# Late loads in fewer, larger pieces without ties, and a new order of work planned with later transpose landings

## The chip, the cores and the metric

The kernel runs on one core of a Trainium2 chip. A core has a matrix engine (TensorE, PE in the profile), a vector engine (VectorE, DVE), an activation engine (ScalarE, ACT), a general engine (GpSimd, POOL) and a queue engine (SyncE, SP) that issues transfers; 16 DMA engines carry them. The metric is the device time of one execution in microseconds (us); smaller is better.

## The reference

One transformer block on a sequence of S = 2048 rows of D = 448 values, in bf16. Six vectors come out of the condition `c`; they shift, scale and gate a memory attention and a gated feed-forward network (FFN). Cut to what matters:

```python
mod = (silu(c) @ w_mod).reshape(1, 6, 1, 448)            # sa, ca, ga, sb, cb, gb
h = layernorm(x) * (1 + ca) + sa
# attention: 16 heads of 28, the sequence in N = 4 segments of L = 512
for s in range(4):
    p = softmax(qs @ ks.T * scale + causal_mask)
    a_dot = p @ vs
    a_mem = (phi(qs) @ M) / (phi(qs) @ z + 1e-6)         # phi(t) = t + 1 if t > 0 else exp(t)
    o = g * a_mem + (1 - g) * a_dot                      # g = sigmoid(beta) of the head
    M = M + phi(ks).T @ vs;  z = z + sum(phi(ks))
x = x + ga * (o @ wo)
h = layernorm(x) * (1 + cb) + sb
x = x + gb * ((sigmoid(h @ w_gate) * (h @ w_up)) @ w_down)   # F = 1792
```

## The kernel before

**Staging.** Everything stays on the core. Rows of x are kept as 16 tiles of 128 rows; four tiles make one segment. Activations that feed a matmul are turned so that the feature lies on the partitions: `hT` holds a segment of the normed input, `qT` and `kT` the projections, `fT` the gated FFN values. A segment passes through `ln1` (layer norm and turning), `proj` (q, k, v), `attention` (logits L962, exponential L976 and L982, causal mask L989 and L992, PV L1017, then `unit`'s vector work), `memory` (phi of k, its transpose L917, the update of M by L925), `wo_ln2` (output projection L1084, second layer norm) and `ffn` (gate and up L1106, tanh L1111, product L1113, down L1125, residual L1132, store L1134).

**Turning.** Segments 1 and 2 of the first layer norm (and segment 0) are turned on TensorE (`turned`). Segment 3 and every second layer norm are turned by DMA transposes on SP (`transposed`, L766), and then two DMA copies, `below` (L783) and `above` (L786), bring the second half-layout of `hT`. `memory` turns phi(k) by a DMA transpose on SP (L917) for segments 0 to 2.

**The order of work is planned.** The kernel first builds a graph of nodes (`add`), one for each group of instructions, with an engine or several possible ones, a duration in ns, its dependencies, and the ring slots it takes and frees. `Graph.run` then walks through time and gives every engine its instructions in a fixed order: of the nodes that are ready, the one with the greatest rank (longest planned path to the end) plus a priority from the table `PRM` goes first. `COST` weighs the durations when a node may go to one of several engines, and `STAY` is a bonus for matmuls of the same kind as the last. On the chip each engine runs its list in that order, and waits where an input is not there yet. What the planner believes only shapes the order; no instruction waits for a planned time.

**The planner's belief about transfers.** A node with `move` bytes extends a modelled queue per issuing engine (`moved`, 215 bytes per ns alone, 111 shared); its result counts as landed when that queue is through, plus `LAND` (800 ns), plus the node's own `lag`. `ready_at` can hold a load of over 100 KB back while the modelled queue is more than `BACKLOG` ahead; at 1e9 it never does. Where the plan leaves TensorE idle, `fillers` adds matmuls that compute nothing needed (L1149), one for each 215 ns of a gap beyond `SLACK`.

**Loads.** The first group (x of segments 0 and 1, w_mod's first two blocks, wq, wk, wv) is issued in a fixed order at the start. The "late" loads follow, all on SP: x of segments 2 and 3, wo, beta, the other four blocks of w_mod, gate and up weights, down weights. They are cut into pieces of mostly 196 to 229 KB. From the 13th load on (`UNTIED`), a load is tied to the third load before it (`DEPTH`): the instruction on SP waits until that one has landed. `ld()` hands out the priorities of the late loads.

```python
        tie = loads[-DEPTH] if len(loads) >= UNTIED else None
        n = add(eng, 450 if size < 200000 else 640, fn, [*deps, tie], prio=prio, use=use, take=take, move=size, lag=lag)
        n.tie = tie
```

**Other names.** `ot` is the ring in which a finished tile of 128 rows waits for its store. w_mod's later blocks are loaded into the `fT` ring's space, blocks 3 and 4 first in it, then 2, then 5; block 2 gives ga, which scales wo (L679, then L757), block 5 gives gb, which scales w_down.

Of the kernel before, what the change touches and what calls it, by code (L numbers as in the profile page):

```python
# [7 lines left out]
BF16 = mybir.dt.bfloat16  # L8
# [5 lines left out]
P = 128  # L14
# [5 lines left out]
BACKLOG = 1e9  # L20
SLACK = 250
# [4 lines left out]
    "ld": (771, 403768, 348483, 259726, 535371, -278835, -292028, 445172, 1332362, 303233, 1310460, 45242, 288244,  # L26
        -128559, 1040237, 258096, -9990, 569649, 1024340, 391761, 273500, 593899, 795982, -203552, 820620, 593017,
        1120207, 330985, 1113461, 774493, -671071, -90668, 539398, 799422, -93184, 23288, -674131, 254991),
    "ws": (-14005, -102989, -62310, -137580, -381981, -699688, -219766, -155414, -94849, -10346, -123259, -3702,
        29063, -36253, -322382, -40930, -239067, -199319),  # L30
    "pj": (-280142, -704069, -638572, -518614, -637310, -994157, -542144, -688882, -109480, 161573, -1121205, 12951,
        -402680, -604681, -789625, -528195, 72916, -492335, 12521, -313241, -475423, 372917, -235992, -493897, 610722,
        658204, 321509, 693085, -400674, -1003709, -194017, 106939, 222219, -486884, 47564, 827879, -632040, 544043,
        -11321, -249733, 478544, -452337, -133586, 492909, 126034),
    "ev": (1516111, 1582287, 1138122, 640813, 1428776, 707733, 1221781, 1425071, 1717384, 1397734, 1614980, 1052150,
        1134267, 1025622, 1180727, 2207166, 1378057, 854006, 1335199, 930050, 1372900, -496693, -46859, 1361141,
        -498332, -673866, 39791, -625676, -211702, -535966, 79681, 418783, -341986, -1205310, -1102479, -1758438,
        -859392, -1109485, -955341, -758887, -1106561, -1044137, -935118, -1085307, -583137, -511278, -1028157,
        -1225711),
    "ln1": (1014613, 259455, 311242, 526284, -532656, 377084, 521927, 458915, 248468, 240899, 80767, 190939, 322045,  # L40
        922394, -153714, 373880, 672893, 684073, 1312461, 646485, 525704, 132711, 142935, 229741, -119849, -25882,
        -1076, 59463, 99488, 4145, 203011, -9620, 36748, -275452, -42630, -532745, 127715, 337951, 124107, 234908,
        173169, 1026151, 293341, -767251, 146664, 291291, -294982, -141991, -214427, -355224, -804385, -231165,
        265245, -289951, 78489, -14810, -607527, 273452, 95473, -109467, -145027, 816731, 184508, -257527, 422111),
    "lg": (3531987, 2928887, 3302070, 2312646, 1981257, 2222351, 1556422, 2079865, 2540545, 1674238, 496386, 1265056,
        644299, 1008454, 803464, 213638, 548428, 1112707, 740179, 279054, 724651, 615799, 812429, 1475696, 1307754,
        581830, 466619, 1033964, 1156072, 857527, 674454, 450311, 546011, 1045955, 595283, 1128384, 850233, 464085,
        496739, 861364),
    "ex": (1660442, 1247168, 1466499, 1378343, 1124806, 556127, 1086877, 940357, 360731, 688715, 2399920, 1680821,
        1560577, 1033906, 1812669, 1303255, 2255484, 2297242, 1801796, 344197, -105916, 575997, 217295, 364760,  # L50
        -144111, 34843, 947142, -243088, -712255, 146737, 1249995, 1295152, 802692, 1243758, 2446324, 1105808,
        1108368, 816977, 1361359, 686920),
    "mask": (2833694, 2172153, 1484862, 2558992, 2745471, 1943529, 1669348, 1566800, 2360084, 2108728, 1848729,
        1771049, 1289664, 2173349, 1689570, 1032184, 372083, 533670, 1070582, 530111, 517237, 567036, 334578, 644150,
        1017921, 1097020, 1263687, 1004873, 761044, 578011, 988940, 1329620, 772189, 530798, 366834, 656439, 773092,
        -452969, 460512, 344381, -382752, 248779, 43481, 1005712, 1163774, 187316, 918710, 863964, -364060, -57999,
        225822, 119677, 455905, 353891, 573582, -336115, 142521, 6226, 871244, 334930, 617018, 447958, 306715,
        823560),
    "pv": (1510960, 2254349, 2150147, 892491, -81679, 241060, 567421, 807042, 479666, 494468, -63278, -109593,
        -365197, -45904, -144814, -682418),  # L60
    "t": (2245238, 2091550, 1479107, 2357610, 2278955, 1940928, 1941447, 2463059, 2054908, 1760115, 1657910, 1666629,
        1715318, 2114714, 1290324, 1855182, 714137, 1869659, 2188586, 1895895, 277605, 932172, 144282, 369456, 432516,
        370017, 275497, -66930, 79936, -66111, 155980, 490864, 995475, 377538, -769977, -593018, 161869, -266693,
        -79670, 112558, 887899, -388864, -721366, -451132, 403656, 179168, 5328, 541028, 1289320, 876258, 1495114,
        1300857, 1661961, 359418, 1176846, 1749849, 530354, 579482, 1179131, 667989, 1127818, 1398569, 890064, 868091,
        1217557, 751753, 1166194, 723957, 1026257, 725394, 1350910, 1100815, 783159, 905073, 764601, 1017372, -918149,
        -347294, -688818, 277986, -73264, -342300, -1164722, -373929, -494748, -249055, -693970, -808798, -932705,
        -1317168, -144432, -1300560, -467191, -376473, -198986, -768635, -951192, -1164539, -833366, -860480, -847331,
        -1205016, -1112039, -972589),
    "mem": (75524, -45857, 9188, 551184, 145444, 51132, 382367, -354439, -82631, 339528, -85643, -352126, -37850,  # L70
        79814, -226912, -49579, 34854, -204535, 646779, -2750, 26526, -54116, 149438, -67183, -123127, -205995,
        551520, -232370, 21817, -17851, 23659, 117299, -297990, -59887, -870756, -180055, 24537, 125755, -319961,
        -313276, 43719, -4031, -195138, 24147, -179664, 373048, 200012, -375, 313049, 240205, -216959, 38022, 78802,
        107419, 111432, 455670, -378853, 59098, 139550, -259246, 424659, -747222, 670979, -62528, 15753, -81855,
        -113175, 2765, -557394, -377468, 395418, 196975, -443658, 319806, -286386, -254599, 284180, 432906, 363582,
        742822, -378872, -14501, 367698, 73066),
    "wo": (1928953, 1133983, 1813540, 2305809, 864403, 1645199, 1747926, 1593145, 691139, 732374, 496645, -54449,
        -926050, 953596, 300390, -140998),
    "ln2": (1235442, 1377352, 1905298, 772371, 1302459, 1454679, 1592833, 713116, 1440875, 1339697, 1170368, 1293312,
        1828436, 1147645, 1699501, 1313252, 1150856, 1235422, 878015, 2046656, 2294705, 2027521, 2032455, 1793018,  # L80
        1744547, 1152936, 853562, 625765, 1526373, 647445, 916507, 962776, 889384, 1328237, 1212566, 918603, 665248,
        648263, 1674146, 408683, 1295773, 1318265, 1064317, 1357524, 885031, 702760, 1493860, 1125808, 819020,
        1311131, 956359, 526544, -1247537, -1766227, -1030854, -1340553, -1669186, -1740353, -1452415, -1159770,
        -847930, -933910, -1364788, -1142350, -1477850, -806597, -1686672, -1416655, -1223326, -1150467, -1728888,
        -1160041, -1823461, -1614144, -1601250, -1685498, -2399938, -1489365, 1616614, 1988001, 2192457, 1853517,
        2476805, 2921069, 1730775, 2573100, 2277872, 2889185, 2711768, 2000762, 2913408, 2496652, 2218550, 2856210,
        2811230, 3473453, 2544526, 2779098, 2604614, 2132813, 2981200, 2286328, 3348949, 2656893),
    "gu": (2673986, 2907356, 2967087, 2529995, 3263422, 2686764, 2603478, 2577456, 1978393, 2148466, 1618981, 1176658,
        2204195, 3478258, 1852084, -121925, 261498, 636554, 209114, 416027, 31833, 498183, 874090, 115018, 221051,
        681715, 442901, 777503, 745824, 803670, -198195, -7556, 1161045, 117077, 681087, 874132, 152642, 541639,  # L90
# [22 lines left out]
        -396451, -551498, -486620, -45176, -808892, -509914, -384534, -367362, -583030, -515930),  # L113
}
STAY = 69838
COST = {"ACT": 0.956, "DVE": 0.949, "POOL": 0.819}


class Slot:
# [225 lines left out]
def kernel(  # L345
# [362 lines left out]
    def ld():  # L708
        return pr("ld", 0)
# [473 lines left out]
```

## Time and profile before

| | us |
|---|---|
| median of 3 runs | 262.75 (261.62 to 262.83) |
| the profiled execution | 261.97 |
| its span, first to last instruction | 260.3 |
| TensorE's mean granted clock | 0.985 |

Busy time of the engines by line, as the profile's groups give it (one row for all shapes of a line's operation):

| line, engine, what | count | busy us | mean ns |
|---|---|---|---|
| L1106 PE gate and up | 784 | 92.3 | 377 |
| L1125 PE down | 224 | 46.3 | 353 |
| L881 PE q and k | 224 | 28.8 | 386 |
| L1149 PE fillers | 14 | 3.9 | 380 |
| L976, L982 ACT exponentials | 40 | 75.4 | 1888, 1879 |
| L1113 DVE product | 56 | 38.1 | 682 |
| L992 DVE masks | 41 | 16.1 | 418 |
| L989 POOL masks | 23 | 14.5 | 638 |

How to read it: matmuls overlap in TensorE's pipeline, so the mean of one is longer than the distance between two. A wait is named as "instruction <- what ended the wait". The DMA transposes L766 and L917 and the copies L783 and L786 have no engine of their own: SP issues them (L917 takes 1.2 us of SP each), and they land later.

When SP issues what, from the timeline: the first group to 9.6 us; x of segment 2 at 15.5; wo from 20.2; w_mod's third block at 23.3; gate and up pieces from 24.9 to 47.7; w_mod's last block at 47.8; the first transpose L917 at 45.8, the others of segment 0 at 53.4, 56.2 and 58.0; down weights from 52.4 to 62.6; the first L766 at 67.4. TensorE's first L1106 starts at 75.1, its first L1125 at 114.7.

### The profile page before, as it was taken

Reading aid. Unit: us, or ns where it says so; the run is one execution under the profiler, and the core shown is the slowest. Engines: PE = TensorE matmul, PEld = TensorE weight load, DVE = VectorE, ACT = ScalarE, POOL = GpSimd, SP = SyncE. Lnnn points to the kernel's source line nnn. Section 1 sums busy time; section 2 is a strip of 40 time slices with the busy share of each in tenths; the row PEclk is TensorE's granted clock in tenths of the full one; section 3 lists DMA queues with packets and bytes.
Section 4 is the critical chain, followed back from the end, with each engine's and each line's share of the span. In section 5 each row is a group of like instructions: output and inputs, shape, how many; then the busy total and the mean of one; then the engine's idle time right before and its main releaser. Section 6 shows DMA issues by size and latency. Waiting matters only on the chain.

```text
span 260.3 us, 6026 instructions
## 1 busy us (share of the span) xinstructions
PE 241.0 (93%) x2397; PEld 107.0 (41%) x2397; DVE 197.4 (76%) x497; ACT 152.6 (59%) x189; POOL 42.6 (16%) x99
## 2 busy tenths in 40 slices
PE   8999699399987989999889999999999999999994
PEld 3634335234423434334335444444444344454442
DVE  4699889779999999998959998589967374342441
ACT  5079878857898775868888863797402310132210
POOL 5215034006401000062001115000011110000000
PEclk9999979989999999999999999999999999999999
DMA  6994776966232041203730001220000014200011
GB/s 165 220 195 110 207 207 191 173 164 165 53 81 61 3 84 40 73 1 77 131 81 0 3 19 24 60 73 18 20 18 0 3 40 100 85 18 3 0 36 37
DMA packets 30088, 19.79 MB, mean 76 GB/s; under 512 B 18603, under 2 KB 28524, under 8 KB 30060
## 3 DMA queue, kind: packets, MB, share of 16 engines
q1 hardware_dynamic: 29532, 18.77, 31.1%
q10 hardware_dynamic: 528, 0.63, 1.0%
q8 instruction: 19, 0.31, 0.5%
q14 instruction: 9, 0.07, 0.1%
HBM read 11.07 MB, written 1.84 MB: 50 GB/s over the span
## 4 chain that ended last, share of the span: by engine, by line
PE 40%; DVE 12%; DMA 3%; issue 1%; POOL 1%; SPq 0%; DVEq 0%
PE ps L1106 23%; PE ps L1125 13%; PE ps L1084 2%; DMA pk<-pq 2%; DMA hT<-hT 1%; DVE fT L1113 1%; DVE aT L1040 1%; DVE x_sb L1087 1%; DVE U L1059 1%; DVE pq L909 1%; DVE A L1044 1%; DVE pT L992 1%; PE ps L1017 1%; DVE st L607 1%; DVE ot L1132 1%
## 5 line engine op out<-in xcount | busy, mean ns | idle before, releaser
L1106 PE MATMUL ps<-hT,wgu 64*128 64x512 bf16 x784 | 92.3, 377 | 2.5 <-DMA hT<-hT 1.8
L1111 ACT ACTIVATE tt<-ps 128x512 f32<-128x512 f32 x56 | 33.5, 597 | 65.5 <-PE ps L1106 64.0
L976 ACT ACTIVATE pT<-ps 128x2048 bf16<-128x2048 f32 x32 | 60.4, 1888 | 8.4 <-PE ps L962 6.3
L1113 DVE SCALAR_TENSOR_TENSOR fT<-tt,ps 128x512 bf16<-128x512 f32 x56 | 38.1, 682 | 29.7 <-ACT tt L1111 29.7
L1106 PEld LDWEIGHTS <-wgu 64*128 64x128 bf16 x784 | 39.0, 94 | 48.9 <-issue 12.5
L1125 PE MATMUL ps<-wd_sb,fT 128*128 128x448 bf16 x224 | 46.3, 353 | 0.4 <-DVE x_sb L1087 0.2
L881 PE MATMUL ps<-hT,wqk 64*128 64x512 bf16 x224 | 28.8, 386 | 2.4 <-DVE hT L841 1.5
L1125 PEld LDWEIGHTS <-fT 128*128 128x128 bf16 x224 | 20.3, 98 | 24.1 <-issue 7.5
L989 POOL TENSOR_SCALAR_AFFINE_SELECT pT<-pT 128x512 bf16<-128x512 bf16 x23 | 14.5, 638 | 92.8 <-DVE pT L992 22.2
L607 DVE BATCH_NORM_STATS2 st<-x_sb 128x6 f32<-128x448 bf16 x32 | 19.6, 614 | 2.8 <-DMA x_sb<-in_A_x_dram 2.4
L881 PEld LDWEIGHTS <-wqk 64*128 64x128 bf16 x224 | 11.1, 95 | 16.5 <-issue 7.1
L615 POOL TENSOR_TENSOR rs<-rs,mhalf 128x1 f32<-128x1 f32 (+1 forms) x29 | 17.2, 591 | 2.4
L982 ACT ACTIVATE pT<-ps 128x2048 bf16<-128x2048 f32 x8 | 15.0, 1879 | 3.6 <-PE ps L962 3.6
L992 DVE TENSOR_TENSOR pT<-pT,cmask 128x512 bf16<-128x512 bf16 x41 | 16.1, 418 | 1.0 <-ACT pT L976 0.7
L962 PE MATMUL ps<-qT,kT 28*128 28x512 bf16 (+3 forms) x256 | 16.0, 302 | 0.4 <-ACT pT L976 0.4
L1132 DVE TENSOR_TENSOR ot<-ps,x_sb 128x448 bf16<-128x448 f32 x16 | 9.9, 616 | 8.2 <-PE ps L1125 5.6
L1084 PE MATMUL ps<-wo_sb,oT 128*128 128x448 bf16 x64 | 13.8, 353 | 0.4 <-DVE M_sb L932 0.3
L614 POOL TENSOR_SCALAR rs<-mv 128x1 f32<-128x1 f32 (+1 forms) x29 | 6.5, 224 | 46.5 <-DVE mv L608 39.4
L893 PE MATMUL ps<-wvv,hT 64*128 64x448 bf16 x112 | 13.1, 378 | 0.0
L909 DVE TENSOR_TENSOR pq<-e 128x512 bf16<-128x512 bf16 x24 | 10.1, 423 | 4.0 <-ACT aT L864 2.1
L1017 PE MATMUL ps<-pT,vt 128*32 128x512 bf16 (+3 forms) x256 | 12.2, 312 | 0.0
L620 DVE TENSOR_SCALAR xn<-x_sb,mv,rs 128x448 bf16<-128x448 bf16 x32 | 10.9, 394 | 1.3 <-POOL rs L615 1.2
(95 smaller groups left out, 237.8 us busy)
## 6 DMA issues: line engine op xcount, KB each, us to landing
out_dram<-ot SPq DMA_DIRECT2D x16, 112.0 KB, 1.7
fT<-in_w_mod_dram SPq DMA_DIRECT2D x8, 196.0 KB, 2.8
wgu<-in_B_w_gate_dram SPq DMA_DIRECT2D x7, 224.0 KB, 3.5
wgu<-in_B_w_up_dram SPq DMA_DIRECT2D x7, 224.0 KB, 3.9
wd_sb<-in_B_w_down_dram SPq DMA_DIRECT2D x7, 224.0 KB, 2.9
x_sb<-in_A_x_dram SPq DMA_DIRECT2D x6, 224.0 KB, 4.3
hT<-hT SPq DMA_DIRECT2D x5, 256.0 KB, 3.7
hT<-hT SPq DMA_DIRECT2D x5, 192.0 KB, 3.4
```

What stands on the lines that cost most here:

```text
L607: nc.vector.bn_stats(st_r[:, st.at, :], src)
L615: nc.gpsimd.tensor_tensor(r, r, mhalf[:, 0:w], ALU.pow)
L881: nc.tensor.matmul(pf(b), lhsT=w, rhs=piece(hT, i, half), start=(i == 0), stop=(i == NP - 1))
L962: nc.tensor.matmul(ps[:, lg.at + hs, o:o + nq], lhsT=kT_r[r, k.at, hcs[u], kb * P:(kb + 1) * P], rhs=qT_r[r, q.at, hcs[u], kb * P:L], star ...
L976: nc.scalar.activation(pT_r[:, pTs[units[0]].at, :, w0:w0 + L], ps_, AF.Exp, scale=scale)
L982: nc.scalar.activation(dst, ps_.rearrange("p h (u w) -> p u h w", u=2), AF.Exp, scale=scale)
L992: nc.vector.tensor_tensor(blk, blk, cmask[:].rearrange("p (o k) -> p o k", o=1).to_broadcast([P, 4, P]), ALU.mult)
L1084: nc.tensor.matmul(pf(b)[:, 0:D], lhsT=oT_r[:, oT.at, k, t * P:(t + 1) * P], rhs=wo_sb[:, k, :], start=(k == 0), stop=(k == NHC - 1))
L1106: nc.tensor.matmul(pf(b), lhsT=wgu[half * HR:(half + 1) * HR, chunk_of(i, half), fs], rhs=piece(hT, i, half), start=(i == 0), stop=(i == N ...
L1111: a = act(485, lambda gp=gp, tt=tt: nc.scalar.activation(tt_r[:, tt.at, :], pf(gp), AF.Tanh, scale=0.5), [n], use=[gp, tt], prio=pr("tanh" ...
L1113: f = dve(597, lambda up=up, tt=tt, ft=ft: nc.vector.scalar_tensor_tensor(fT_r[:, ft.at, :], tt_r[:, tt.at, :], 1.0, pf(up), op0=ALU.add, ...
L1125: nc.tensor.matmul(pf(b)[:, 0:D], lhsT=fT_r[:, fts[fc].at, t * P:(t + 1) * P], rhs=wd_sb[:, fc, :], start=(fc == 0), stop=(fc == NFC - 1))
```

## The change

It does six things:

1. The late loads are cut into fewer, larger pieces (22 instead of 38), in another list order: x of segment 2 in one piece, w_mod block 2 before wo, then wo, beta, blocks 3 and 4 in one piece, all gate and up weights in eight pieces, x of segment 3, block 5, and the down weights in four.
2. `UNTIED` goes from 13 to 999, so that no load waits for another's landing. Instead the planner holds a load back, in the plan only, while its modelled queue is over 4 us ahead (`BACKLOG`).
3. Planned landings are later: L766 by 0.4 us, L783 and L786 by 0.4, L917 by 2.6 in segment 0 and by 0.4 in the others. L1132 gets a planned lag of 1.5 us except in the last segment.
4. The ring `ot` has four places instead of two.
5. `SLACK` for fillers falls from 250 to 150 ns.
6. All priorities in `PRM`, and `STAY` and `COST`, have new values, so the order on every engine is a new one. Nothing that is computed changes.

```diff
-BACKLOG = 1e9
-SLACK = 250
+BACKLOG = 4000
+SLACK = 150
...
-STAY = 69838
-COST = {"ACT": 0.956, "DVE": 0.949, "POOL": 0.819}
+STAY = 116271
+COST = {"ACT": 0.94, "DVE": 1.373, "POOL": 0.932}
...
-    ot_r = ring("ot", 2, [P, D], BF16)
+    ot_r = ring("ot", 4, [P, D], BF16)
...
-    DEPTH, UNTIED = 3, 13
+    DEPTH, UNTIED = 3, 999
...
-    load_x("SP", 2 * TPS, 2 * TPS + 2, ld())
-    load_x("SP", 2 * TPS + 2, 3 * TPS, ld())
+    load_x("SP", 2 * TPS, 3 * TPS, ld())
+    load_wm(("SP",), 2, 1, fT_flat[:, 2 * NK * D:], ld())
     l_wo = [load("SP", wo_sb[h * HP:h * HP + Dh, :, :], A_wo.rearrange("(c h e) n -> h e c n", h=4, e=Dh)[h],
                  Dh * NHC * D * 2, [n_wopad], prio=ld()) for h in range(4)]
     l_beta = load("SP", beta_row[:], A_beta.rearrange("(o h) -> o h", o=1), 40, prio=ld())
-    load_wm(("SP", "SP"), 2, 1, fT_flat[:, 2 * NK * D:], ld)
-    W_gu = []
-
-    def load_gu(c0, c1):
-        for c in range(c0, c1):
-            W_gu.extend(load_half("SP", wgu, half, w, ld(), c, c + 1) for half, w in ((0, B_w_gate), (1, B_w_up)))
-    load_gu(0, 2)
-    load_wm(("SP",) * 4, 3, 2, fT_flat, ld)
-    load_gu(2, 4)
-    load_x("SP", 3 * TPS, 3 * TPS + 2, ld(), [n_warm, n_pads, *n_vpad, *n_vone, *n_opad])
-    load_x("SP", 3 * TPS + 2, 4 * TPS, ld(), [n_warm, n_pads, *n_vpad, *n_vone, *n_opad])
-    load_gu(4, NC)
-    load_wm(("SP", "SP"), 5, 1, fT_flat[:, 3 * NK * D:], ld)
+    load_wm(("SP",), 3, 2, fT_flat, ld())
+    W_gu = [load_half("SP", wgu, half, w, ld(), c0, c1) for c0, c1 in ((0, 2), (2, 4), (4, 6), (6, 7))
+            for half, w in ((0, B_w_gate), (1, B_w_up))]
+    load_x("SP", 3 * TPS, 4 * TPS, ld(), [n_warm, n_pads, *n_vpad, *n_vone, *n_opad])
+    load_wm(("SP",), 5, 1, fT_flat[:, 3 * NK * D:], ld())
     l_wd = []
-    for f0 in range(0, NFC, 2):
-        l_wd += [load("SP", wd_sb[:, f0:f0 + 2, :], B_w_down.rearrange("(fc p) n -> p fc n", p=P)[:, f0:f0 + 2, :],
-                      2 * P * D * 2, W_p if f0 < NC else (), prio=ld())] * 2
+    for f0, f1 in ((0, 4), (4, 7), (7, 11), (11, 14)):
+        l_wd += [load("SP", wd_sb[:, f0:f1, :], B_w_down.rearrange("(fc p) n -> p fc n", p=P)[:, f0:f1, :],
+                      (f1 - f0) * P * D * 2, W_p if f0 < NC else (), prio=ld())] * (f1 - f0)
...
-        return add("SP", 1305, fn, [n], use=[xn, hT], prio=prio, move=60000, lag=400)
+        return add("SP", 1305, fn, [n], use=[xn, hT], prio=prio, move=60000, lag=800)
...
-        xs = [add("SP", 530, below, hs[0:NK - 1], use=[hT], prio=prio(), move=80000, lag=900),
-              add("SP", 600, above, hs, use=[hT], prio=prio(), move=80000, lag=1000)]
+        xs = [add("SP", 530, below, hs[0:NK - 1], use=[hT], prio=prio(), move=80000, lag=1300),
+              add("SP", 600, above, hs, use=[hT], prio=prio(), move=80000, lag=1400)]
...
-                pk_r[:, pk.at, :, :], pq_r[:, f2.at, :]), [n], take=[pk], use=[f2], move=60000, lag=400, prio=pr("mem", s))
+                pk_r[:, pk.at, :, :], pq_r[:, f2.at, :]), [n], take=[pk], use=[f2], move=60000, lag=3000 if s == 0 else 800, prio=pr("mem", s))
...
-                                                                         ALU.add), [n], take=[ot], use=[b, op], prio=pr("ot", s))
+                                                                         ALU.add), [n], take=[ot], use=[b, op], prio=pr("ot", s),
+                    lag=1500 if s + 1 < NSEG else 0)
```

Of `PRM`, which has 20 rows of priorities in the planner's ns, the first numbers of the row for the late loads show the kind of change:

```diff
-    "ld": (771, 403768, 348483, 259726, 535371, -278835, -292028, 445172, 1332362, 303233, 1310460, 45242, 288244,
...
+    "ld": (848832, 1133906, 790932, 1270633, 1125054, 925640, 883939, 769965, 722178, 891683, 726716, 704550, 662251,
...
```

## The prediction

> **What bounds the kernel now.** I read the page's first two parts, then the engines by stretches, then TensorE's waits, then the timeline around the longest of them.
>
> ```profile
> PE 241.0 (93%) x2397; PEld 107.0 (41%) x2397; DVE 197.4 (76%) x497; ACT 152.6 (59%) x189; POOL 42.6 (16%) x99
> ...
> PE   8999699399987989999889999999999999999994
> ...
> DVE  4699889779999999998959998589967374342441
> ...
> PEclk9999979989999999999999999999999999999999
> DMA  6994776966232041203730001220000014200011
> GB/s 165 220 195 110 207 207 191 173 164 165 53 81 61 3 84 40 73 1 77 131 81 0 3 19 24 60 73 18 20 18 0 3 40 100 85 18 3 0 36 37
> ```
>
> PE is busy 241.0 of 260.3 us. The digits (6.5 us each) show two halves: from about 150 us PE has no gap to the end, while DVE falls to 2 to 7; before 80 us PE has its gaps and its two low clocks (slices 6 and 9), and DVE stands at 8 to 9. So the end is fixed by PE's total work plus what PE loses early, and DVE is the second bound of the early part. The DMA engines carry loads until slice 10, at 207 GB/s at best and 110 at worst.
>
> ```profile
> 15.40:23.20 7.80, 7.80 (x80) 3.39 (x78) 7.47 (x19) 6.87 (x10) 3.69 (x10) 1.00 0.61 141
> 23.20:44.00 20.80, 18.21 (x219) 8.19 (x214) 18.84 (x57) 17.29 (x19) 5.92 (x12) 0.92 0.71 196
> 44.00:56.00 12.00, 7.67 (x114) 3.85 (x110) 9.05 (x26) 7.67 (x9) 0.13 (x1) 0.86 0.87 175
> 56.00:62.60 6.60, 6.25 (x65) 2.72 (x66) 6.33 (x19) 4.80 (x8) 2.95 (x5) 1.00 0.68 177
> 62.60:80.00 17.40, 14.57 (x197) 5.91 (x193) 16.95 (x48) 16.32 (x19) 5.31 (x11) 1.00 0.32 74
> ```
>
> Columns: stretch, length, then PE, PEld, DVE, ACT, POOL busy, PE's granted clock, DMA share, GB/s. PE idles 80 - 68.24 = 11.8 us in the first 80 (their sum row), and 19.3 in all; 3.5 of that is the drain at the very end. The worst stretch is 44 to 56: 4.3 us idle at a clock of 0.86.
>
> ```profile
> PE ps L925 <- DMA pk<-pq: 4.3, 1, 4.3
> PE ps L881 <- DVE hT L841: 1.5, 1, 1.5
> PE ps L1106 <- DMA hT<-hT: 1.3, 1, 1.3
> ...
> PE ps L679 <- DMA fT<-in_w_mod_dram: 1.0, 1, 1.0
> ```
>
> That is TensorE's list of waits in the first 80 us (total, times, longest). One wait of 4.3 us, for the transpose of phi(k) of segment 0, is over a third of the idle time. Its place:
>
> ```profile
> 45.81 1.30 SPq L917 DMA_TRANSPOSE pk<-pq  x1
> ...
> 47.78 2.75 SPq L478 DMA_DIRECT2D fT<-in_w_mod_dram  x2
> ...
> 51.46 0.30 PE L925 MATMUL ps<-vt,pk 128*32 128x32 bf16 x16 [4.33 <-DMA pk<-pq]
> ...
> 51.69 2.80 PE L893 MATMUL ps<-wvv,hT 64*128 64x448 bf16 x14
> ```
>
> SP issues the transpose at 45.81 and it lands at about 51.4, 5.6 us later, where the median transpose lands in 2.4 (when no loads run). Behind the waiting L925 stood work that was ready: these 14 matmuls of L893 read the hT of segment 1, made by 34.5 us.
>
> **The change, part by part.** The sum is made against the profiled execution, 261.97 us (its span 260.3 and 1.67 around it); the median of the shown runs is 262.75, 0.78 more.
>
> *Loads.* After the first group the late loads are 2 x 0.459 (x) + 0.401 (wo) + 0.401 + 0.803 + 0.401 (w_mod) + 3.211 (gate, up) + 1.606 (down) = 7.74 MB, before and after. The 38 issues become 22. The ties go. SP then needs, at 0.75 us for a large piece (the mean of the two 392 KB issues of wvv) and 0.33 for each of wo's, 16 x 0.75 + 1.3 + 0.2 = 13.5 us: from 9.6 us, where it now begins to wait, it could be through at 23 instead of 62.6, except for loads that the plan puts behind a transpose. The engines can't follow: 3.33 MB of first loads at 195 GB/s end at 17.1 us, 7.74 MB at 196 (the row 23.2 to 44) take 39.5, so the last load lands at about 56.6 instead of 65. What waits for a load on PE now: 1.0 us at L679, for w_mod's third block. It moves ahead of wo's four small pieces (SP spends 2.5 us on them, in the 110 GB/s slice) and is no longer tied; I credit 0.5 of the 1.0, since DVE is busy 4.29 of 5 us there and is late next. The gate, up and down weights are first read at 75 and 114, long after they land in both versions: earlier is worth nothing there.
>
> *Transposes behind loads.* [...] The row: with at most three pieces in flight, the transpose took 5.6 us instead of 2.4, so 3.2 us of queue. [...] But the plan is told: for segment 0 the landing is set at 3.0 us + 0.8 (LAND) + 0.28 (its own bytes) + the planned backlog of up to 4.0 (BACKLOG; one large piece, 2.1, more just after a load) behind its issue of 1.3, so up to 9.4 us from its start, 55.2 for a start at 45.8. PE's fixed order then puts other work ahead of L925. I take the plan's side, since not all loads stand ahead of a transpose that SP reaches at 46 (ten stand behind it now). What is gained: at most 4.33 idle and the low clock beside it, 12 x 0.14 = 1.7, together 6.0; at least what DVE can follow. DVE idles 12 - 9.05 = 2.95 in that stretch, and fills 90% or more of the next two, so I take **-3.0**. Below zero: the rival below.
>
> *The clock.* [...] The row of 23 to 44 has 0.92 though its longest wait is 1.5 us (L881 after L841), so shorter waits, close together, cost it too: 20.8 x 0.08 = 1.7 us. [...] I take the row, and have it inside the -3.0.
>
> *Shift copies and other transposes.* Planned landings grow by 0.4 us (L766, L783, L786, and L917 after segment 0). L783 and L786 land 3.4 and 3.7 us from their issue; the old plan had 2.6 and 2.8 (0.53 or 0.60 + 0.37 + 0.8 + 0.9 or 1.0), the new 3.0 and 3.2. PE waited 1.8 for them, twice: 2 x 0.4 could go, and I take **-0.4**, since something else must be ready there.
>
> *SLACK 250 to 150.* Five gaps got 14 fillers (L1149, 3.9 us busy). 100 ns more admits a further 215 ns filler in 47% of gaps: 2 to 4 more, nothing where PE idles anyway, 0.8 where it doesn't: **+0.3**.
>
> *The ot ring of 4.* It ends one wait of 2.4 us of DVE for a store. No wait of PE ends with it, as PE is full of FFN matmuls then: 0; if that cover were thin, up to -0.4 (L1106 after L1132).
>
> *COST and priorities.* DVE is priced 1.373 instead of 0.949, so an evacuation goes to ACT unless ACT is busy for 0.38 us more (before 0.11), and a mask to POOL unless DVE comes free within 0.13 (before 0.20). One evacuation moved takes 0.68 from DVE and gives ACT 0.59; one mask 0.42 and gives POOL 0.64. Ten of each would take 11 us from DVE, but ACT has only 0.4 to 2.2 us free in each 10 us from 20 to 50. No trace of before shows the new order. Bounds: all of PE's idle time and lost clock before 80 us (11.8 + 3.4, so -15) and new waits as large as today's (+8). I take 0, because the old plan was likewise searched and its order loses little outside the named places.
>
> Sum: -3.0 - 0.5 - 0.4 + 0.3 = -3.6; 261.97 - 3.6 = **258.4 us**.
>
> **The rivals.** *A, the queue decides (slower).* SP runs far ahead and every late load stands before the first L917. At 175 GB/s (the row 44 to 56) the loads end at 17.1 + 44.2 = 61.3 and the transpose lands at 63.7; PE arrives at the planned 55.2 and waits 8.5, so 4.2 more than now, with 1 us more of low clock: 262 + 5 = **267**. It decides from a landing after 59.5 (55.2 + today's 4.3). For it: 24 GB/s is seen around transposes, and the plan counts on 215 bytes per ns, which no slice but the second reaches. Against: the 3.0 us. *B, new waits elsewhere (slower).* ACT is busy 9.58 of 10 us at 20 to 30 and 9.85 at 70 to 80, and gets more work by COST. An exponential (1.9 us) that is late for want of ACT holds the PV matmuls and the segment behind it; two such, before FFN matmuls can stand in, are 262 + 4 = **266**. Against it: PE waits 1.2 us for ACT today (rows of 0.5, 0.4 and 0.3). *C, DVE was the bound* and the freed time is lost in the next stretch: **262**. *D, the relief of DVE works*: half of the 15 us goes: **254**.
>
> **How the numbers follow.** Forecast (256 to 261.3) 0.40, D 0.12, C 0.09, A 0.25, B 0.14. Measurement tells 0.5%, 1.3 us, from no change: faster 0.52, same 0.09, slower 0.39. The likeliest case's own range is 256 to 261.3; to hold 8 in 10 it must take in most of A, B and D: 253 to 269.
>
> **What would show it.** Right: the loads end near 57 us; the wait of L925 for pk falls below 1.5 us; the clock of 44 to 56 is above 0.95; the first L1106 comes 2 to 4 us before 75. Wrong: a wait of L925 above 4.3 us, first L1106 at 75 or later, or ACT's waiting work holding PE (waits for L976, L864) by more than 2 us. The forecast fails if the new order loses time where this profile names none.

## The result, and the profile after

| | before | after |
|---|---|---|
| median, us (4 runs each) | 262.79 (261.62 to 263.92) | 258.99 (258.85 to 259.67) |
| the profiled execution | 261.97 | 258.85 |
| its span | 260.3 | 257.1 |
| TensorE's mean granted clock | 0.985 | 1.000 |

The ratio of the times is 0.9861 (95% interval 0.9814 to 0.9907): faster by 1.4%. The forecast was 258.4, its range 253 to 269. Ratios and intervals, here and below, leave out the slow executions (those over 1.5% above the fastest of their kernel), while medians are of all, so a ratio can differ from that of the medians beside it. Lines of the new kernel behind its loads stand nine lower (L1106 is L1097, L925 is L916).

The page's first two parts of after: busy time by engine, then the forty slices, now of 6.4 us.

```profile
PE 241.6 (94%) x2407; PEld 107.7 (42%) x2407; DVE 193.6 (75%) x486; ACT 155.9 (61%) x194; POOL 48.1 (19%) x105
...
PE   8987899897889999999899999999999999999994
...
DVE  4788699999999999998998999898944343333341
...
PEclk9999999999999999999999999999999999999999
DMA  5999999971333523004312000022343000110011
```

Both low clocks are gone. DVE does 3.8 us less (197.4 before), ACT 3.3 and POOL 5.5 more. Half of the layer norm's last step, `hT` times scale plus shift (L778 before, L769 and L767 now), went over: before, all 20 of these ran on DVE; now 10 do, 5 run on ACT and 5 on POOL. PE's idle time fell from 19.3 to 257.1 - 241.6 = 15.5 us; ten more fillers (24 instead of 14) hide part of what is left.

The same stretches as before the change (length, then PE, PEld, DVE, ACT, POOL busy, PE's clock, DMA share, GB/s):

```profile
15.40:23.20 7.80, 6.63 (x60) 2.62 (x61) 6.57 (x18) 6.44 (x10) 2.74 (x8) 1.00 1.14 200
23.20:44.00 20.80, 18.99 (x258) 9.16 (x254) 18.17 (x55) 18.54 (x21) 5.72 (x12) 1.00 1.11 205
44.00:56.00 12.00, 10.88 (x169) 5.36 (x167) 11.62 (x32) 11.94 (x14) 0.63 (x1) 1.00 1.05 237
56.00:62.60 6.60, 5.40 (x40) 2.11 (x38) 6.20 (x17) 3.10 (x4) 3.29 (x6) 1.00 0.21 42
62.60:80.00 17.40, 15.02 (x180) 6.94 (x177) 16.76 (x47) 16.13 (x18) 6.49 (x12) 1.00 0.34 58
```

The stretch 44 to 56 holds 169 matmuls at full clock instead of 114 at 0.86, and DVE is now busy 11.62 of its 12 us, ACT 11.94. The loads end near 56: 237 GB/s up to there, 42 behind it. TensorE's own waits in the first 80 us (total, times, longest):

```profile
PE ps L702 <- DVE x_sb L554: 1.2, 1, 1.2
PE ps L1008 <- DVE hT L832: 1.1, 1, 1.1
PE ps L678 <- DMA fT<-in_w_mod_dram: 0.9, 1, 0.9
...
PE ps L872 <- DVE M_sb L925: 0.8, 1, 0.8
```

The wait of 4.3 us for the transpose of phi(k) is gone. But the first FFN matmul, which was to come 2 to 4 us before 75, comes later than before (75.1), between fillers (L1141); the timeline of TensorE:

```profile
73.76 1.47 PE L1141 MATMUL ps<-ident 128*128 128x512 bf16 x6
75.25 0.40 PE L953 MATMUL ps<-qT,kT 28*128 28x384 bf16 x8
76.02 0.93 PE L1097 MATMUL ps<-hT,wgu 64*128 64x512 bf16 x6 [0.38 <-DVE hT L769]
76.89 1.25 PE L1141 MATMUL ps<-ident 128*128 128x512 bf16 x5
```

**Where the time was won.** Busy time can't tell: six matmuls of one shape are 1.11 us of it in before (L1106 at 75.11) and 0.93 in after (L1097 at 76.02), at a clock of 1.00 in both. So I counted TensorE's useful work done by a time T: matmuls ended by then, each by the distance between two starts of its shape at full clock, fillers left out. The total is 221.2 us in both kernels.

| T, us | 44 | 56 | 62.6 | 80 | 130 | 150 | 170 | 230 |
|---|---|---|---|---|---|---|---|---|
| before | 27.7 | 34.0 | 39.9 | 53.2 | 99.6 | 117.0 | 135.6 | 194.6 |
| after | 28.8 | 38.8 | 43.9 | 53.5 | 99.3 | 118.2 | 137.7 | 197.5 |
| lead | 1.1 | 4.8 | 4.0 | 0.3 | -0.3 | 1.2 | 2.1 | 2.9 |

The stretch that I argued from gives a lead of 4.8 us at 56, more than forecast, and all but 0.3 of it is spent by 80. The lead that lasts opens behind 130. This counts TensorE alone: behind 130 VectorE has 82.1 us of work left in before and 77.7 in after, some of it done or passed on earlier, some passed to ACT and POOL later (before first):

```profile
130.00:260.30 130.30, 124.85 (x1067) 55.26 (x1063) 82.08 (x177) 56.53 (x71) 11.34 (x24) 1.00 0.13 32
130.00:257.10 127.10, 123.45 (x1014) 54.19 (x1012) 77.74 (x166) 52.23 (x68) 12.71 (x26) 1.00 0.13 32
```

There VectorE had also waited in before (its waits of 60 to 180 us: total, times, longest):

```profile
DVE fT L1113 <- ACT tt L1111: 3.0, 4, 1.6
DVE pq L909 <- ACT aT L864: 2.1, 1, 2.1
DVE hT L778 <- DMA hT<-xn: 1.2, 2, 0.9
DVE pq L909 <- DMA pk<-pq: 0.9, 1, 0.9
```

In its timeline (start, length, instruction, and the idle time before it) the two of L909 stand close together:

```profile
131.82 0.42 DVE L909 TENSOR_TENSOR pq<-e 128x512 bf16<-128x512 bf16 x1 [0.85 <-DMA pk<-pq]
...
136.39 0.43 DVE L909 TENSOR_TENSOR pq<-e 128x512 bf16<-128x512 bf16 x1 [2.15 <-ACT aT L864]
```

L909 makes phi of a half of q or k in the ring `pq`, which has three places. A place with a half of k comes free when the transpose that reads it has landed. The second wait is put down to ACT, but the transpose of the place before it was issued at 132.30 and landed at 136.27; that is what ended it. In after the same list has 1.9 us for places in `pq`, two waits, and 1.5 instead of 3.0 for ACT's tanh (the first row).

### The profile page after: what moved, and what is told of

Read it like the earlier page. It is cut to its first block, busy times and chain, and to the rows that moved or that the text cites. A ratio compares the mean times of both kernels' runs of the same rounds, so it can differ in the third digit from the quotient of the medians.

```text
span 257.1 us, 6034 instructions
## 1 busy us (share of the span) xinstructions
PE 241.6 (94%) x2407; PEld 107.7 (42%) x2407; DVE 193.6 (75%) x486; ACT 155.9 (61%) x194; POOL 48.1 (19%) x105
## 4 chain that ended last, share of the span: by engine, by line
PE 58%; DVE 11%; DMA 3%; issue 1%; ACT 0%; DVEq 0%
PE ps L1097 32%; PE ps L1116 15%; PE ps L1075 4%; PE ps L953 2%; PE ps L1008 2%; DMA pk<-pq 2%; PE ps L872 2%; DMA hT<-hT 1%; DVE pT L983 1%; DVE A L1035 1%; DVE U L1050 1%; DVE pq L900 1%; DVE fT L1104 1%; PE ps L1023 1%; DVE aT L857 1%
## 5 line engine op out<-in xcount | busy, mean ns | idle before, releaser
L1097 PE MATMUL ps<-hT,wgu 64*128 64x512 bf16 x784 | 92.2, 377 | 1.5 <-DMA hT<-hT 0.5
L1097 PEld LDWEIGHTS <-wgu 64*128 64x128 bf16 x784 | 38.5, 94 | 49.2 <-issue 11.9
L980 POOL TENSOR_SCALAR_AFFINE_SELECT pT<-pT 128x512 bf16<-128x512 bf16 x22 | 13.8, 636 | 58.8 <-DVE O L1056 18.2
L983 DVE TENSOR_TENSOR pT<-pT,cmask 128x512 bf16<-128x512 bf16 x42 | 17.1, 435 | 1.3 <-ACT pT L967 1.0
L872 PEld LDWEIGHTS <-wqk 64*128 64x128 bf16 x224 | 11.3, 94 | 14.3 <-issue 4.6
```

Of the source, the lines that this page charges most:

```text
L872: nc.tensor.matmul(pf(b), lhsT=w, rhs=piece(hT, i, half), start=(i == 0), stop=(i == NP - 1))
L983: nc.vector.tensor_tensor(blk, blk, cmask[:].rearrange("p (o k) -> p o k", o=1).to_broadcast([P, 4, P]), ALU.mult)
L1097: nc.tensor.matmul(pf(b), lhsT=wgu[half * HR:(half + 1) * HR, chunk_of(i, half), fs], rhs=piece(hT, i, half), start=(i == 0), stop=(i == N ...
```

## The experiments

Theories. **P**: the wait of L925 for the transpose was the loss, as forecast. **A**: untying the loads lengthens the transposes (my slower rival). **T**: the ties themselves cost time. **V**: VectorE sets the pace to 150 us, and its waits and work decide. Ratios are to the kernel before, with 95% intervals; runs that were timed together share its runs, with medians of 263.14 (the first four), 262.30 (the next four) and 263.71 (the last four). Line numbers shift by a few in each kernel.

**1. Before, with the first L925 moved.** It and its two vector steps stand three PE nodes later; all else keeps its order.

```diff
+        group = [n for n in order if n.tag == first.tag]
...
+        after = [n for n in rest[at0:] if n.eng == "PE"][2]
+        i = rest.index(after) + 1
+        order = rest[:i] + group + rest[i:]
```

> The kernel before, its order kept except that the first update of M (L925 for the first head group of segment 0, with its two small VectorE steps) stands three TensorE nodes later, behind 14 matmuls of v, the PV of one unit and the block of ga. Theory P (the early wait of TensorE for the transpose is what the change wins): the 4.3 us wait falls below 2 us and the time falls by 2 to 3 us. Theory V (VectorE paces everything from 20 to 150 us, and the change wins by giving VectorE less work and fewer waits there): the wait falls as much, but TensorE runs out of work before its first FFN matmul near 75 us, and the time falls by less than 0.7 us.

Measured: 1.0002 (0.9964 to 1.0039), 263.14 us. TensorE's waits of 40 to 80 us:

```profile
PE ps L901 <- ACT pT L986: 2.0, 1, 2.0
PE ps L687 <- DMA fT<-in_w_mod_dram: 1.5, 1, 1.5
PE ps L1116 <- DVE hT L786: 1.3, 2, 1.0
```

The wait for the transpose is gone, and others of 2.0 and 1.5 us stand in its place; VectorE then waits 3.5 us for L933, the moved matmul (its list of 40 to 140 us). So taking that wait away by order alone is worth nothing here in the mean. It isn't a clean test of P, since the move starves VectorE. The 2.0 us also tell that the 14 matmuls behind L925 (L901 here) were not ready: they wait for an exponential of ACT, which ends at 48.11. In before that exponential is 1 us later:

```profile
47.25 1.88 ACT L976 ACTIVATE pT<-ps 128x2048 bf16<-128x2048 f32 x1 [0.37 <-PE ps L962]
```

So of the wait of 4.33 us, 47.13 to 51.46, about 51.46 - 49.13 = 2.3 us could be filled with them (an estimate from these two traces). The executions differ with the clock: five ran at 0.992 or 0.993 and took 260.5 to 261.9 us, the other seven at 0.972 to 0.987 took 262.9 to 265.9.

**2. Before, without ties.**

```diff
-            if n.tie is not None:
+            if False and n.tie is not None:
```

> The kernel before with the same plan and order, and no load tied to another's landing on the chip. Rival A of the prediction (queue): loads run ahead, the first transpose of phi(k) lands later than 51.4 us, its wait grows from 4.3 to 8 us or more, and the time grows by 2 to 5 us. Theory V: the wait may grow by a few us, but VectorE has other work there, so the time changes by less than 1 us. If the ties themselves cost time: loads end near 57 us instead of 65 and the time falls by over 1 us.

Measured: 0.9918 (0.9886 to 0.9949), 260.49 us. A predicted a longer wait. SP's timeline:

```profile
34.43 0.47 SPq L478 DMA_DIRECT2D wgu<-in_B_w_gate_dram  x1
44.08 1.30 SPq L917 DMA_TRANSPOSE pk<-pq  x1
45.43 0.58 SPq L478 DMA_DIRECT2D wgu<-in_B_w_up_dram  x1
```

What SP waits for between 30 and 50 us:

```profile
SPq L917 <- DVE aT L866: 9.4, 1, 9.4
```

And PE's timeline where the transpose is read:

```profile
48.39 0.28 PE L925 MATMUL ps<-vt,pk 128*32 128x32 bf16 x16 [2.25 <-DMA pk<-pq]
```

SP runs ahead, and then stands 9.4 us at the transpose itself, whose input isn't made. Every load behind it in SP's list waits too. By 42 to 44 us the DMA engines are empty (last two numbers of the first stretch):

```profile
42.00:44.00 2.00, 2.00 (x33) 0.79 (x30) 1.97 (x6) 1.27 (x3) 1.15 (x2) 1.00 0.00 0
...
50.00:52.00 2.00, 2.00 (x20) 0.75 (x19) 1.93 (x7) 1.47 (x3) 0.00 (x0) 0.50 0.70 214
```

So the transpose meets no queue: issued at 44.08 instead of 45.81, landed 4.3 us later instead of 5.6. A falls; T holds, with 0.8%. (The second line shows the clock at 0.50 behind the wait of 2.25 us.)

**3. Before, with more places for phi.** The plan still reckons with three; the places are handed out in turn, `pq` over five and `pk` over four.

```diff
-    pq_r = ring("pq", 3, [P, L], BF16)
-    pk_r = ring("pk", 3, [P, TPS, P], BF16)
+    pq_r = wide("pq", 3, 5, [P, L], BF16)
+    pk_r = wide("pk", 3, 4, [P, TPS, P], BF16)
```

> The kernel before, same order on every engine; only the rings pq (3 to 5 places) and pk (3 to 4 places) are larger, so that VectorE's phi product and SyncE's transpose wait less for a place. Theory V: VectorE's two waits at 131 and 134 us (0.85 and 2.15 us) go, and the time falls by 1.5 to 3 us. Theory P: those waits are off TensorE's path and the early wait of 4.3 us stays, so less than 0.5 us.

Measured: 0.9926 (0.9885 to 0.9968), 261.17 us. VectorE's two waits of 131 to 137 us are gone (those for ACT's exponentials grow from 0.7 to 1.9 us), while TensorE still waits 3.2 for the early transpose. Useful work is 118.6 at 150 us, like after's 118.2. A wait of VectorE that TensorE's list hardly shows is worth 0.7%: for V, with both rings widened at once.

**4. After, with ties.** Each late load waits for the second load issued before it on SP, not the third, as the text below has it: `issued` already holds the load itself when `[-3]` is taken. In the trace the load at 29.84 leaves when the one at 24.79, two before it, lands (29.82). So these ties are tighter than before's, in pieces about twice as large.

```diff
+            if n.late:
+                tc.add_manual_dep(block[was], issued[-3], mybir.DependencyInfo(
```

> The changed kernel, same plan and order, each late load tied on SyncE to the landing of the third load issued before it. If loads without ties are what the change wins: loads end later than 60 us and the time grows by 1 us or more towards 262. Theory V: loads end later, nothing but block 2 of w_mod is waited for, and the time changes by less than 0.7 us.

Measured: 1.0072 (1.0042 to 1.0101), 264.44 us, against 0.9861 for after: ties this tight cost some 2.1%. One wait begins it, in PE's timeline:

```profile
36.77 0.82 PE L661 MATMUL ps<-silu,fT 112*128 112x32 bf16 x16 [4.36 <-DMA fT<-in_w_mod_dram]
```

The load that it waits for, in SP's timeline:

```profile
29.84 0.60 SPq L480 DMA_DIRECT2D fT<-in_w_mod_dram  x1
```

w_mod's blocks 3 and 4 are issued at 29.84 instead of 21.61 in after, and TensorE (4.4 us) and VectorE (4.3, behind L661) both wait for them. An order that was planned for early loads needs them early.

**5 and 6. Before, with dummy work.** Ten memsets of a scrap tile on DVE, or ten pairs of fillers on PE, spread over 58 to 114 us of the plan. Nothing reads them.

```diff
+            if n.eng == "DVE" and extra and n.start >= extra[0]:
+                extra.pop(0)
+                self.spare()
```

> The kernel before, same order, with ten extra writes of zeros to a scratch tile on VectorE (128 x 400 float32, some 0.4 us each, 4 us in all), one every 6 us of the plan from 58 to 114 us. They compute nothing that is used. Theory V (VectorE paces until about 150 us): the time grows by 3 to 4 us. Theory P (TensorE paces from its first FFN matmul on): less than 1 us.

> The kernel before, same order, with twenty extra filler matmuls (0.215 us each, 4.3 us in all) on TensorE, two at a time over the same stretch of the plan as in the run with extra VectorE work. They compute nothing that is used. Theory P: the time grows by about 4 us. Theory V in its strong form: less than 2 us. If both this run and that one grow by 3 us or more, the two engines are equally near the bound, and only a loss on both or on the one that is later at that moment counts.

Measured: 1.0119 (1.0087 to 1.0151), 265.29 us, for VectorE, and 1.0052 (1.0017 to 1.0087), 263.81 us, for TensorE. The group of the memsets (count, then busy us and mean ns):

```profile
L1157 DVE MEMSET scrap<- 128x400 f32 x10 | 3.9, 392 | 0.3
```

3.9 us of DVE cost 0.0119 x 262.30 = 3.1 us, 0.8 for each (0.6 to 1.0 by the interval); 4.3 us of PE cost 0.0052 x 262.30 = 1.4 us, 0.3 for each (0.1 to 0.5). In this stretch it is mainly VectorE, 76% busy over the whole span, that sets the pace, not the engine that is 93% busy.

**7. Before, with the modulation shared.** Two of each four steps of L778 are bound to POOL and ACT; the order stays.

```diff
+            hs[-1].tag = {1: "POOL", 3: "ACT"}.get(kc)
```

> The kernel before, same order, with half of the 20 modulation steps after the DMA transposes (L778) taken from VectorE: in each group of four the second runs on GpSimd and the fourth on ScalarE, 4 us less on VectorE in all, 2.5 us of it before 130 us. Theory V: the time falls by 1 to 2.5 us. Theory P: no change beyond 0.5 us, or slower by up to 1 us since GpSimd takes 0.77 where VectorE takes 0.41.

Measured: 1.0088 (1.0045 to 1.0130), 263.97 us: slower, though it takes as many steps from VectorE as the change does. TensorE's waits of 60 to 120 us:

```profile
PE ps L1111 <- DMA hT<-hT: 1.5, 1, 1.5
PE ps L1111 <- POOL hT L782: 1.0, 1, 1.0
```

POOL took 0.77 us for such a step in after (DVE 0.41), and these steps feed the shift copies and the first FFN matmuls. Less work on VectorE isn't enough by itself: a step moved to a slower engine needs an order that starts it earlier.

**8. After, with the modulation back on DVE.**

```diff
+        for n in order:
+            if n.tag == "mod":
+                n.eng = "DVE"
```

> The changed kernel, same order, with the ten modulation steps that its plan gave to ScalarE and GpSimd (L767, L769) put back on VectorE: 4 us more there in all, 2 us of it before 130 us. Theory V: the time grows by 1 to 2.5 us, so about half of what the change won is lost. Theory P: less than 0.5 us.

Measured: 0.9958 (0.9927 to 0.9989), 260.75 us. Against after's 0.9861, whose interval it doesn't meet (each beside its own runs of before), about 1%, or 2.5 us, is lost (0.4 to 1.5% by the two intervals). In the new order the offload is worth that.

**9. Before, untied and with more places.** Edits 2 and 3 together, on the old order.

> The kernel before, same order, with two edits together: no load tied on the chip, and rings pq of 5 and pk of 4 places. If what the change wins is fewer waits in the early half, on VectorE above all, the two parts add: ratio to the kernel before 0.984 to 0.988, the same as the changed kernel's 0.986, without any new plan. If the two remove the same loss, 0.991 to 0.993 like each alone; then the rest of the gain belongs to the new plan.

Measured: 0.9799 (0.9756 to 0.9841), 258.52 us; its profiled span is 255.8. The two gains add (0.9918 x 0.9926 = 0.9845 was to be expected from them), and here the first FFN matmul does come early, in PE's timeline:

```profile
71.47 1.11 PE L1116 MATMUL ps<-hT,wgu 64*128 64x512 bf16 x6
```

Useful work at 80 us is 57.0, against 53.2 before and 53.5 after; at 150 it is 120.8. The old order, with a line taken out and two rings widened, gains no less, as far as the intervals tell, than the new order with all its numbers.

**10, 11 and 12. After, with one thing changed.** `pq` with four places; no fillers; every late load of over 300 KB issued as two halves.

```diff
+    pq_r = wide("pq", 3, 4, [P, L], BF16)
...
+SLACK = 1e9
...
+            if late and size > 300000:
+                h = dst.shape[1] // 2
+                q.dma_start(dst[:, 0:h, :], src[:, 0:h, :])
+                q.dma_start(dst[:, h:, :], src[:, h:, :])
```

> The changed kernel, same order, with a fourth place in the ring pq (3 to 4). VectorE's two waits for a place after 100 us (1.09 and 0.76 us, 1.9 in all) should go. If VectorE paces that stretch: ratio to the kernel before 0.979 to 0.982, the first version to beat both. If the new plan has work enough beside them: 0.985 to 0.988, as the changed kernel.

> The changed kernel, same order, without any of its 24 filler matmuls (5.2 us of TensorE). If the fillers are what keeps the granted clock at 1.00: the clock falls below 0.99, as in the kernel before, and the time grows by 1 to 3 us. If they only fill idle time of a stretch that VectorE paces: clock 0.99 or more and the time within 0.5 us. If some stand in the way: faster by up to 2 us.

> The changed kernel, same order, with each late load of over 300 KB issued as two halves one after the other, so 15 more issues and pieces as small as before, none tied. If the size of the pieces matters for itself: loads end later than 58 us and the time grows by 0.5 to 1.5 us. If only the ties mattered: within 0.5 us.

Measured: 0.9797 (0.9739 to 0.9856), 0.9861 (0.9804 to 0.9918) and 0.9781 (0.9739 to 0.9822); medians 259.45, 260.81 and 257.72 us. Against after's 0.9861 none is settled: the intervals meet, and after itself was not timed beside them. But the halves give no sign that large pieces are what wins: half the size is no worse. Without the fillers the first sign that I had named came: all six executions ran at a clock of 0.961 to 0.987, where three of after's four had 1.000 and one 0.986. In the profiled one, the slowest (264.00 us), the clock of the first 44 us was 0.84 (after: 1.00):

```profile
0.00:44.00 44.00, 38.39 (x385) 19.04 (x389) 30.55 (x95) 25.46 (x38) 13.15 (x41) 0.84 1.05 180
```

So the fillers do hold the clock; what that is worth in time is not settled, with after's ratio but a median of 260.81 us against its 258.99. The halves and the fourth place for `pq` have, with experiment 9, the lowest ratios of all the kernels here, and are what I would try together next; that was not run.

## Why the prediction was right or wrong

The total was right, in sign and size: 261.97 - 3.6 = 258.4 forecast, 258.85 in the profile. The steps behind it were right in part, and their errors cancelled, so that the closeness of the total is in good part luck.

**The wait of L925, -3.0: the event right, its worth wrong.** The wait went, the clock of 44 to 56 rose from 0.86 to 1.00, and the loads ended near 56 (56.6 forecast): three of the four signs. The fourth, a first L1106 2 to 4 us before 75, failed: it came at 76.0, and "first L1106 at 75 or later" was one of my signs of being wrong. One step that failed is "work that was ready": by experiment 1 the 14 matmuls could fill about 2.3 of the 4.33 us. The other is "at least what DVE can follow": I took DVE's idle 2.95 us in that stretch as time it could give. DVE filled it (11.62 of 12), PE led by 4.8 us at 56, and by 80 the lead was 0.3: the first FFN matmul waits for `hT` from DVE, and fillers stand ahead of it and behind. As I read it, PE had run ahead of a chain over DVE and ACT that its early matmuls don't shorten. Rival C (the freed time is lost in the next stretch) describes this place; I gave it 0.09. Experiment 1 agrees as far as it goes: without that wait, no gain in the mean. I had also misread VectorE's row: it falls to 3 to 7 only behind some 189 us; from 150 to there it reads 9, 8, 5, 8, 9, 9, so VectorE stays close to the bound for longer than I said.

**The ties, -0.5: too small.** I credited only the wait for w_mod's block 2, and that one hardly changed (1.0 to 0.9). Untying is worth 0.8%, some 2.2 us, on the old order; on the new one ties tighter than before's cost 2.1%. I priced the ties by PE's waits for loads alone; what they did was to let SP come late to everything behind them, transposes included. That the ties were free to remove was argued against by rival A, in which the first transpose lands behind all the late loads, at 63.7 us. That was an estimate of mine, and no run shows it. It left out that SP goes through its list in order: it stands at a transpose until the input is made (9.4 us in experiment 2), so that few bytes can be ahead (there none: 0 GB/s from 42 to 44 us). In after SP waits the same way; from its list of 20 to 60 us:

```profile
SPq L908 <- DVE pq L900: 9.2, 2, 6.6
SPq L908 <- DVE R L1043: 8.9, 1, 8.9
SPq L908 <- DMA fT<-in_w_mod_dram: 2.7, 2, 1.5
...
SPq L477 <- DMA wvv<-in_A_wv_dram: 1.9, 1, 1.9
```

Its timeline:

```profile
21.61 0.60 SPq L477 DMA_DIRECT2D fT<-in_w_mod_dram  x1
...
26.55 1.30 SPq L908 DMA_TRANSPOSE pk<-pq  x1
27.90 0.63 SPq L477 DMA_DIRECT2D wgu<-in_B_w_gate_dram  x1
...
30.86 0.61 SPq L477 DMA_DIRECT2D wgu<-in_B_w_up_dram  x1
40.56 1.23 SPq L908 DMA_TRANSPOSE pk<-pq  x1
```

The first transpose now leaves at 26.55, with five loads issued behind it and then none until the second, 9 us on; it leaves some 14 us ahead of the matmul that reads it (40.21, no wait). I was right to take the plan's side, for a reason I only half gave.

The last row of the list shows a second limit, which I had not seen: "no load waits for another's landing", as I described the change, is not so. The load at 21.61 left when wvv's second half, issued at 10.72, landed at 21.60. In experiment 2, whose loads have no ties either, SP's list of 20 to 60 us has loads waiting 1.6 us for a landing of x and 0.9 for one of the gate weights; why they wait was not measured. Nor did all 7.74 MB stand ahead of a transpose, as rival A has it: ten of the 22 late loads left ahead of the first, and twelve behind it. And SP was not through at 23 us: the last three late loads left from 46.84 on. (That sum counts 16 large pieces where the list has 17, so 14.3 us and not 13.5; nothing else hung on it.)

**COST and priorities, 0 between -15 and +8: wrong, but inside.** Experiment 8 puts the modulation's offload at about 1% in the new order; DVE's waits of 3.0 us for places in `pq` became 1.9. I saw DVE as "the second bound of the early part" and then credited its relief with nothing. Of the ten steps passed on, five lie between 92 and 127 us, near where experiment 5 took its price: 5 x 0.41 x 0.8 make 1.6 us, and the other five, behind 177, have no price. That estimate is worked out, not shown: experiment 7 has the same relief and loses.

**Shift copies, -0.4:** PE's wait for L1106 by the copies went from 1.8 us in all to 0.5. The direction was right and the size a third; part of it may be the new order. **SLACK, +0.3:** ten more fillers, where I had 2 to 4; no cost was found, and without any the clock was 0.961 to 0.987 (experiment 11). **The ot ring, 0:** DVE's wait of 2.4 us for a store is gone; no run isolates it. **The later planned landings** weren't isolated either: with one number changed the planner gives another order throughout, so such a run would compare two orders.

**The clock.** I took the row of 23 to 44, 0.92 with no wait above 1.5 us, as a sign that waits shorter than the one of 4.33 us cost clock too. That was right: 0.50 followed a wait of 2.25 us in experiment 2. After has no wait above 1.2 us in its first 80 us and a clock of 1.00 throughout. But the freed clock lies ahead of 56 us, where little of the lead lasted. Is the clock alone the gain? After's one execution at 0.986 took 259.02 us, no more than the three at 1.000 (258.85 to 259.67); experiment 8 ran nine of its twelve at 0.997 or more and gains 0.4%; experiment 9 gains 2.0% at 0.987 to 0.993. So it is not the whole. It does count: of before's 32 executions beside experiments 1 to 4, the 13 at 0.984 to 0.987 had a median of 262.0 us, the 13 at 0.978 to 0.981 one of 263.7.

What stays open is how the gain of after divides between untied loads, less work on VectorE and the rest of the order. Experiment 8 shows that it needs the second and experiment 4 that it does not bear tight ties, and experiment 9 that the old order gets about as much from untied loads and a wider ring; these don't add up to a split.

## What to carry to other kernels

The busiest engine need not be the one that sets the pace: put a few microseconds of dummy work on each engine in turn and see how much of it reaches the end (here 0.8 on VectorE, 0.3 on TensorE). Before crediting a stall that goes, see whether the work behind it was ready, follow the lead to the next thing that must be ready, and compare useful work done by a time T instead of idle time. Look at short rings on the pacing engine and at what an in-order issuing queue stands waiting for, because a wait there holds back everything that is listed behind it (9.4 us in experiment 2).

## What the runs showed of the hardware that was not expected

The granted clock fell to 0.50 after a single TensorE wait of 2.25 us (experiment 2: 46.1 to 48.4 us idle, a clock of 0.95 in 48 to 50, 0.50 in 50 to 52 and 0.70 in 52 to 54), and in the kernel before after one of 1.5 us, as its stretches of 2 us show:

```profile
32.00:34.00 2.00, 1.38 (x10) 0.40 (x9) 2.00 (x7) 1.63 (x2) 0.00 (x0) 0.97 0.79 224
34.00:36.00 2.00, 2.00 (x24) 0.74 (x22) 1.67 (x5) 1.65 (x1) 1.26 (x3) 0.50 0.74 206
36.00:38.00 2.00, 2.00 (x27) 0.84 (x26) 1.41 (x4) 0.90 (x3) 1.17 (x2) 0.68 0.84 234
```

The wait ended at 32.54; the low clock begins 1.3 us behind it, at 33.88, over a busy PE, so it is easily charged to the wrong place.

In experiment 2 a low clock also follows shorter waits. From 71 to 77 us TensorE waits 0.35, 1.00, 0.25 and 0.46 us; from 77.04 on 22 FFN matmuls take 4.37 us, where before does 21 in 2.53 (79.98), and the clock of 56 to 80 us is 0.87.

And the first transpose of experiment 2 was slow with no loads ahead of it: the DMA engines moved 0 GB/s in the two microseconds from 42 to 44, and it still took 4.3 us from its issue at 44.08, with loads issued behind it, where the median one of before takes 2.4.
